# Attention and a two-matrix FFN on one core: batch 2's q and k taken from fp16 copies in DRAM by transposed loads, with a new order of steps

## The chip, the cores and the metric

One of the eight cores of a Trainium2 chip runs the kernel. The metric is the device time of one execution in microseconds. A core has a matrix engine (TensorE, PE in the profile; its weight loads are PEld), VectorE (DVE), ScalarE (ACT), GpSimd (POOL) and SyncE (SP), which run side by side, each taking its own instructions in program order. POOL, SP and ACT also issue the transfers between DRAM and the on-chip memory, which 16 DMA engines carry out.

## The reference

```
scores = (q @ k^T) / 8                        # 8 batches, 12 heads, 448 tokens, 64 channels
attn   = exp(scores) / (1 + sum exp(scores))  # as it comes out: the maximum cancels
x      = (attn @ v), heads side by side       # 3584 tokens x 768
out    = relu(x @ w_in)^2 @ w_out             # w_in 768 x 2048, w_out 2048 x 768
```

All inputs and the output are float32 in DRAM. The kernel computes in fp16 with float32 sums.

## The kernel before

The scores of a head need q and k with the 64 channels on partitions. They come by two ways. Batches 0, 1 and 2 (`ON_PE`) are loaded in their natural form, four heads at a time (a "quad" g: heads 2g, 2g+1, 2g+6 and 2g+7, so three quads to a batch), with a cast to fp16 in the load (`load_quad`, POOL's queue). TensorE transposes each quad of q or k in 14 instructions (`transpose_one`, step `T`), and DVE or ACT copies the result out of PSUM into the batch's tile `qk` (`transposed_copy`, step `U`). Batches 3 to 7 go through DRAM: `stage(b)` (POOL's queue) casts a batch of q and of k into the fp16 buffers `stage_q` and `stage_k`, and `transposed_loads(b)` (SP's queue) reads them back transposed into three planes of `qk`: q, k, and k shifted by one row, so that two tokens stand side by side on the 128 partitions. `tail_keys(b)` then gathers each head's last keys with four POOL copies into `flatq`. `qk` has two buffers, so a batch's planes take the place of the planes of two batches earlier.

A visit of `quad_scores` (step `s`) makes 64 keys' scores for the four heads of a quad against all 448 queries: four matmuls of 448 columns for a batch of `ON_PE`, eight of 224 for the others. `quad_exp` (`e`) is the exponential on ACT, `add_quad` (`a`) sums on DVE, `sums_of_quad` (`S`), `quad_z` (`Z`) and `quad_reciprocal` (`M`) make the denominator, `values_step` (`v`) multiplies with v and `quad_x` (`X`) writes x. The scores go through two PSUM buffers, so a visit waits for the exponential of the visit two before it. Batch 0 does the same in halves of 224 queries, with steps of its own (`p` for the values, `y` for the sums, `z`, `n`, `x`); visits 0 to 23 are batch 0's, 24 to 44 batch 1's, 45 to 65 batch 2's. The first FFN product is `half_in` (`i`) for batch 0 and `later_in` (`j`) for the rest, `relu` (`r`, `k`) and `squared` (`g`, `l`) follow, and `out_piece` (`o`) with `out_done` (`O`) or `out_first` and `out_second` (`O`, `Q`) make and store the output.

There are no loops that schedule: the string `ORDER` lists the steps from the start to the end of batch 2's attention, and `CYCLE` lists those of one batch, run for b = 3 to 7. In both, each word is a step letter with its arguments, and each engine executes its share in the order of the string. A short tail follows.

`d` in ORDER issues an entry of the list `LOADS`: natural quads (0 to 7), v quads of batches 0 and 1 (8 to 13), v of batch 2 (14), `win` in four pieces of two loads (15 to 18), `wout` in four (19 to 22), `stage(3)` (23) and `load_third` (24), which is `transposed_loads(3)`, `tail_keys(3)`, v of batch 3 and `stage(4)`. All but the transposed loads stand in POOL's queue, in the order of the string. In CYCLE a single `d0`, near the end, does this for the next batches:

```
def following():
    if b + 1 < B:
        transposed_loads(b + 1)
        tail_keys(b + 1)
        load_v_quads(b + 1)
        if b + 2 < B:
            stage(b + 2)
```

Most matmuls are recorded under one helper line, L92 (`mm`); L198 are the transposes of `T`, L245 the exponentials, L208 and L206 the copies of `U`, L163 the transposed loads, L179 the copies of `tail_keys`, L154 the staging loads, L116 the natural quads, L104, L102 and L110 the loads of v, L134 `win`, L138 `wout`, L531 the output stores.

Of the kernel before, what the change touches and what calls it, by code (L numbers as in the profile page):

```python
# [16 lines left out]
def kernel(  # L17
# [142 lines left out]
    def transposed_loads(b):  # L160
        qk = qks[b] = qk_pool.tile([128, 3, COLS], FP16, name="qk")
        for i, n, x, c in ((0, "q", FRONT, H * S // 2), (1, "k", FRONT, H * S // 2), (2, "k", 0, COLS)):
            nc.sync.dma_start(  # L163
                out=qk[:, i, 0:c],
                in_=stages[n, b][x:x + c * 2 * D].rearrange("(r c) -> r c", c=2 * D),
                transpose=True,
            )
# [494 lines left out]
    ORDER = """
        d0 W8 c1,4,0 c0,0,1 c1,0,1 t0,0,0 c0,4,1 t1,0,0 u0,0,0,0 t1,0,4 u1,0,0,0 t0,0,4 u1,0,4,0 s0 d8 d1 u0,0,4,0 t0,1,0 e0 t1,1,0 u0,1,0,0 u1,1,0,0 s1 s2 e1
        d10 t0,1,4 u0,1,4,0 t1,1,4 u1,1,4,1 T0,1,0 T0,1,1 s3 U0,1,0,0,4,0 e2 U0,1,1,0,4,0 s4 U0,1,0,4,7,1 e3 d9 U0,1,1,4,7,0 d2 p0 e4 p2 s16 p1 e16 b0,0 b0,1
        p3 b0,2 b0,3 s6 y0 d18 s5 T0,2,0 e6 U0,2,0,0,4,0 z0 T0,2,1 U0,2,1,0,4,0 e5 U0,2,1,4,7,0 U0,2,0,4,7,0 s7 s9 b1,0 n0 b1,1 e7 x0 s8 p4 e9 b1,2 d3 b1,3 p5
        e8 p6 p7 s10 y1 b2,0 p8 p9 e10 s11 p10 b2,1 z1 e11 b2,2 b2,3 s12 p11 s13 n1 x1 y2 e12 T1,0,0 U1,0,0,0,7,0 T1,0,1 z2 n2 s14 e13 x2 p12 p13 s15
        U1,0,1,0,7,0 e14 e15 s17 p14 b3,0 b3,1 e17 s18 i0,7 d17 d5 b3,2 e18 b3,3 p15 y3 z3 b4,0 r0,7,0 s21 s19 e21 T1,1,1 d4 n3 b4,1 i0,6 U1,1,1,0,7,0 s20 d15
        T1,1,0 x3 b4,2 e19 b4,3 d16 s23 p16 p17 p18 r0,6,0 U1,1,0,0,7,0 e20 b5,0 e23 s22 e22 b5,1 p19 y4 s26 z4 n4 i0,4 g0,7 x4 r0,4,0 s27 i0,5 g0,6 b5,2 e26
        s25 e27 T1,2,1 s28 e25 p20 p21 r0,5,0 p22 s24 g0,5 b5,3 e28 d11 T1,2,0 p23 e24 s29 y5 e29 U1,2,1,0,7,0 U1,2,0,0,7,0 T2,0,0 T2,0,1 U2,0,0,0,7,0 z5 g0,4
        d6 U2,0,1,0,7,0 s30 n5 s32 a0,0 e30 d13 i0,0 i0,1 s33 x5 e32 r0,0,0 g0,0 r0,1,0 s31 i1,0 d12 g0,1 e33 i0,3 r1,0,0 e31 r0,3,1 s35 d7 s36 e35 P0 e36  # L670
        i0,2 s34 e34 a0,1 a0,2 g1,0 v0,0 a0,3 S0 v0,1 v0,2 v0,3 v0,4 Z0 v0,5 v0,6 M0 r0,2,0 g0,3 g0,2 s37 i1,3 a1,0 a1,1 e37 X0 r1,3,0 a1,2 g1,3 i1,6 s39 s40
        a1,3 e39 i1,1 r1,1,0 r1,6,0 s43 T2,2,0 e40 d20 T2,2,1 g1,6 e43 s42 g1,1 e42 U2,2,0,0,7,0 s41 d19 i1,5 r1,5,0 e41 s38 e38 T2,1,0 T2,1,1 U2,2,1,0,7,0
        U2,1,0,0,7,1 S1 a2,0 Z1 s44 U2,1,1,0,7,0 i1,4 i1,2 a2,1 e44 r1,4,1 s45 a2,2 g1,5 a2,3 v1,0 v1,1 M1 v1,2 v1,3 v1,4 v1,5 v1,6 r1,2,1 v2,0 S2 v2,1 X1
        g1,4 e45 g1,2 v2,2 v2,3 v2,4 Z2 v2,5 v2,6 M2 s47 X2 s46 i1,7 j3,0,2 r1,7,0 o0,0,4 j3,2,4 j1,0,2 j3,4,6 k3,0 j12,0,2 o0,4,8 j1,2,4 o0,8,12 e46 e47
        o0,12,16 s50 d21 g1,7 s51 j12,2,4 j1,4,6 k1,0 j5,0,2 e51 e50 l3 j5,2,4 j5,4,6 d23 O0,1 k5,1 j12,4,6 l5 o1,0,4 s48 s49 j6,0,2 e49 l1 e48 d22 k12,1 l12
        o1,4,8 o1,8,12 o1,12,16 s53 s52 e52 e53 j6,2,4 j10,0,2 o5,0,4 j6,4,6 O1,1 s55 k6,0 s54 j10,2,4 o5,4,8 j0,0,2 e55 a3,0 j10,4,6 j8,0,2 o5,8,12 j0,2,4
        a3,1 k10,1 o5,12,16 e54 s61 s57 l6 a4,0 j14,0,2 O5,0 e57 j14,2,4 j14,4,6 e61 j8,2,4 a3,2 j9,0,2 j9,2,4 j0,4,6 j9,4,6 a3,3 j8,4,6 l10 s56 k0,0 k14,0
        e56 l0 k8,1 s58 o2,0,4 o2,4,8 l14 d14 s59 v4,0 v4,1 v4,2 v4,3 a4,1 v4,4 v4,5 e58 k9,0 s60 e59 s64 o2,8,12 d24 l9 o2,12,16 a4,2 a4,3 j7,0,2 e60 v4,6
        e64 S4 Z4 M4 O2,0 S3 j7,2,4 o4,0,4 l8 o4,4,8 o4,8,12 o4,12,16 j7,4,6 Z3 s62 X4 s63 M3 O4,0 v3,0 v3,1 v3,2 v3,3 v3,4 v3,5 e62 v3,6 s65 X3 k7,1 j4,0,2
        e65 o3,0,4 a5,0 o3,4,8 o3,8,12 o3,12,16 j15,0,2 j4,2,4 j4,4,6 l7 e63 j15,2,4 a5,1 j2,0,2 O3,1 a5,2 j2,2,4 a5,3 j15,4,6 k4,0 j13,0,2 j11,0,2 S5 Z5  # L680
        k15,0 M5 l4 l15 j2,4,6 k2,0 j13,2,4 l2 j11,2,4 j13,4,6 j11,4,6 k11,1 k13,1 l11 l13
    """
# [35 lines left out]

    CYCLE = """
# [5 lines left out]
        e3,1 o4,2,4 o6,14,16 s3,2 e3,3 o4,4,6 O6,1 a2,2 o4,6,8 s3,5 a2,3 o4,8,10 Q6 o4,10,12 e3,2 e3,5 o4,12,14 o4,14,16 O4,1 Q4 a3,0 s3,6 v2,0 v2,1
        S2 Z2 v2,2 v2,3 v2,4 v2,5 M2 v2,6 e3,6 X2 j2,0,2 j2,2,4 j2,4,6 k2,0 j13,0,2 j13,2,4 l2 j13,4,6 j3,0,2 k13,1 l13 j3,2,4 j15,0,2 j12,0,2 j15,2,4
        j0,0,2 j3,4,6 a3,1 j15,4,6 k3,1 a3,2 k15,1 j12,2,4 a3,3 l15 j0,2,4 j0,4,6 l3 j12,4,6 j10,0,2 j10,2,4 j4,0,2 k0,0 l0 k12,1 l12 j10,4,6 j6,0,2
        j7,0,2 j7,2,4 j7,4,6 j4,2,4 k10,0 j6,2,4 j4,4,6 l10 j6,4,6 k7,1 j5,0,2 l7 j5,2,4 k4,1 j11,0,2 k6,0 j11,2,4 j11,4,6 j9,0,2 l6 j5,4,6 l4 j9,2,4
        j8,0,2 j8,2,4 k5,1 j9,4,6 l5 j1,0,2 k11,0 j8,4,6 j1,2,4 j1,4,6 k9,1 j14,0,2 j14,2,4 l11 l9 k8,0 j14,4,6 l8 k1,1 l1 k14,0 S3 Z3 d0 l14 M3
# [61 lines left out]
```

## Time and profile before

| | |
|---|---|
| median of 3 runs | 396.51 us (396.07 to 397.43) |
| the profiled execution, its own time | 396.87 us |
| its span, first to last instruction | 394.8 us |
| PE busy | 385.5 us, 98% |
| DVE / ACT / POOL busy | 240.5 / 238.1 / 59.8 us |
| transposes of `T` on TensorE (L198) | 224, of them 84 for batch 2 |
| HBM read / written | 45.69 / 17.93 MB |
| granted TensorE clock | 1.00 |

The page gives busy times of each engine, the chain of work that ended last, followed back from the last instruction, and the costliest groups of instructions. The timeline lists instructions in order of time; a row has start, length, engine, line, operation, what is written and read, and in brackets the idle time before it and what ended it. The DMA view lists the queues (q0 is POOL's queue, q1 SP's) with packets, megabytes and the time that their packets took as a share of 16 engines, and the issues with the time from issue to landing. The windows view gives for a stretch the busy time and instruction count of each engine (PE, PEld, DVE, ACT, POOL), the granted clock, the DMA engines' share and GB/s (bytes as written). A busy PE isn't PE at its peak, since matmuls overlap: a step's cost is read from start to start.

### The profile page before, as it was taken

To read this page: it belongs to the slowest core of one execution; us is meant where nothing else is said; L and a number is where in the kernel's file an instruction comes from. 1 tells how busy PE (TensorE), PEld (TensorE's weight loads), DVE (VectorE), ACT (ScalarE), POOL (GpSimd) and SP (SyncE) were. 2 spreads that over 40 slices of the span, in tenths; PEclk is the share of its full clock that TensorE was granted. 3 is DMA by queue.
4 is the path that set the end of the run, shared out by engine and by line. 5 is a ranking of instruction groups with operands and counts; after the bars stand their busy time and mean duration, and the time that the engine had idled before them with its cause. 6 is when DMAs were issued, how large, how long until landed. Compare 5 with 4: busy or idle time off the path is not lost.

```text
span 394.8 us, 13877 instructions
## 1 busy us (share of the span) xinstructions
PE 385.5 (98%) x6252; PEld 262.9 (67%) x6252; DVE 240.5 (61%) x445; ACT 238.1 (60%) x324; POOL 59.8 (15%) x96
## 2 busy tenths in 40 slices
PE   8789999999999999999999999999999999999997
PEld 4567776445599766896579866776677765555665
DVE  3889994385746765668536876567646785285000
ACT  4999895768479625895279834896269934100111
POOL 8354500003200032000500016000500000000000
PEclk9999999999999999999999999999999999999999
DMA  8999999568942579419692398527652100100222
GB/s 146 203 204 206 203 206 208 98 127 154 191 85 63 113 140 181 96 43 161 113 203 75 77 193 127 129 64 141 126 74 68 58 7 2 62 0 14 68 80 81
DMA packets 75051, 45.33 MB, mean 115 GB/s; under 512 B 47472, under 2 KB 72944, under 8 KB 74992
## 3 DMA queue, kind: packets, MB, share of 16 engines
q0 software_dynamic: 24752, 22.62, 36.3%
q1 hardware_dynamic: 49952, 21.59, 25.0%
q8 instruction: 49, 0.80, 0.8%
q10 hardware_dynamic: 288, 0.23, 0.2%
q14 instruction: 10, 0.08, 0.1%
HBM read 45.69 MB, written 17.93 MB: 161 GB/s over the span
## 4 chain that ended last, share of the span: by engine, by line
PE 94%; DVE 3%; ACT 1%; issue 1%; DVEq 0%; ACTq 0%
PE mp L92 81%; PE sp L92 9%; PE xp L92 2%; PE mp L198 2%; ACT et L245 1%; DVE qk L208 1%; DVE half L334 1%; DVE half L332 0%; PE mp L225 0%; ACT rcp L356 0%; ACT rcp L363 0%; DVE qk L235 0%; DVE half L338 0%; DVE half L336 0%; DVE rt L496 0%
## 5 line engine op out<-in xcount | busy, mean ns | idle before, releaser
L92 PE MATMUL mp<-wout,gs 64*64 64x384 f16 (+2 forms) x2592 | 166.7, 322 | 0.0
L92 PE MATMUL mp<-xt,win 128*64 128x448 f16 (+2 forms) x1344 | 151.4, 339 | 0.1
L245 ACT ACTIVATE et<-sp 128x896 f16<-128x896 f32 (+1 forms) x131 | 110.8, 889 | 30.1 <-PE sp L92 28.9
L92 PEld LDWEIGHTS <-win 128*64 128x64 f16 (+1 forms) x1344 | 89.6, 106 | 58.7 <-issue 7.4
L92 PEld LDWEIGHTS <-gs 64*64 64x64 f16 (+1 forms) x2592 | 105.9, 106 | 34.3 <-issue 1.1
L494 ACT ACTIVATE rt<-mp 128x448 f16<-128x448 f32 x55 | 29.3, 544 | 57.2 <-PE mp L92 52.4
L500 DVE TENSOR_TENSOR gs<-rt 128x448 f16<-128x448 f16 x128 | 49.2, 401 | 22.2 <-ACT rt L494 19.8
L92 PE MATMUL sp<-qk 64*64 64x224 f16 (+1 forms) x1056 | 57.4, 274 | 2.5 <-issue 0.9
L496 DVE TENSOR_SCALAR rt<-mp 128x448 f16<-128x448 f32 x73 | 45.2, 621 | 23.0 <-PE mp L92 21.5
L557 ACT ACTIVATE ot<-mp 128x384 f32<-128x384 f32 (+2 forms) x34 | 16.4, 481 | 51.3 <-PE mp L92 50.8
L92 PEld LDWEIGHTS <-qk 64*64 64x64 f16 x1056 | 36.1, 114 | 14.4 <-issue 7.4
L179 POOL COPY flatq<-qk 64x384 f16<-64x384 f16 x20 | 12.4, 643 | 205.9 <-DMA qk<-stage_k 205.6
L245 ACT ACTIVATE nn<-sp 128x896 f16<-128x896 f32 x42 | 36.7, 915 | 1.9 <-PE sp L92 1.8
L478 DVE TENSOR_TENSOR xt<-mp,rcp 128x448 f16<-128x448 f32 x42 | 24.3, 620 | 20.0 <-ACT rcp L457 17.8
L92 PEld LDWEIGHTS <-vn 64*64 64x64 f16 x756 | 24.1, 107 | 9.8 <-issue 2.6
L563 DVE SCALAR_TENSOR_TENSOR ot<-mp,ot 128x384 f32<-128x384 f32 x35 | 19.5, 556 | 16.9 <-ACT ot L557 15.3
L454 ACT ACTIVATE rcp<-sp,one_b 128x896 f32<-128x896 f32 x21 | 21.2, 1007 | 10.0 <-PE sp L92 10.0
L92 PE MATMUL mp<-et,vn 64*64 64x448 f16 (+1 forms) x448 | 25.1, 343 | 0.0
L559 DVE TENSOR_SCALAR ot<-mp 128x384 f32<-128x384 f32 x23 | 12.8, 556 | 19.6 <-PE mp L92 19.5
L432 DVE TENSOR_TENSOR half<-et 128x1792 f16<-128x1792 f16 x15 | 16.3, 1087 | 7.0 <-ACT et L245 6.9
L457 ACT ACTIVATE rcp<-rcp 128x896 f32<-128x896 f32 x21 | 20.0, 952 | 0.6
L434 DVE TENSOR_TENSOR half<-half,et 128x1792 f16<-128x1792 f16 x15 | 16.4, 1091 | 0.7 <-ACT et L245 0.3
(59 smaller groups left out, 198.2 us busy)
## 6 DMA issues: line engine op xcount, KB each, us to landing
out_dram<-ot SPq DMA_DIRECT2D x52, 96.0 KB, 2.3
out_dram<-ot SPq DMA_DIRECT2D x19, 192.0 KB, 1.9
win<-in_moe_w_in_dram POOLq DMA_DIRECT2D x8, 384.0 KB, 11.1
wout<-in_moe_w_out_dram POOLq DMA_DIRECT2D x4, 768.0 KB, 15.6
vn<-in_v_dram POOLq DMA_DIRECT2D x10, 288.0 KB, 4.8
stage_q<-in_q_dram POOLq DMA_DIRECT2D x4, 676.0 KB, 8.8
stage_k<-in_k_dram POOLq DMA_DIRECT2D x4, 676.0 KB, 12.0
nn<-in_q_dram POOLq DMA_DIRECT2D x8, 224.0 KB, 8.1
```

The source lines that it names most:

```text
L92: return nc.tensor.matmul(out_, lhsT, rhs, start=start, stop=stop)
L245: nc.scalar.activation(out=out_, in_=in_, func=AF.Exp, scale=scale)
L432: nc.vector.tensor_add(esq[m], a[:, 0:w], a[:, w:2 * w])
L434: nc.vector.tensor_add(esq[m], esq[m], z[:, 0:w])
L454: nc.scalar.activation(out=rcp, in_=zp[:, :, 0:S], func=AF.Ln, bias=one_b)
L457: nc.scalar.activation(out=zqs[m], in_=zqs[m], func=AF.Exp, scale=-1.0)
L478: nc.vector.tensor_mul(xts[b][:, 2 * g + i, :], xqs[m][i][:, 0:S], zqs[m][:, i, :])
L494: nc.scalar.activation(out=rt[:, 0:m], in_=hp[:, 0:m], func=AF.Relu)
L496: nc.vector.tensor_scalar(out=rt[:, 0:m], in0=hp[:, 0:m], scalar1=0.0, scalar2=None, op0=ALU.max)
L500: nc.vector.tensor_mul(gs[:, f0:f0 + per, t0 % RING:t0 % RING + n], r, r)
L557: nc.scalar.activation(out=ot, in_=op[:, 0:w], func=AF.Copy, scale=OUT_SCALE)
L563: nc.vector.scalar_tensor_tensor(out=ot, in0=lo[:, 0:w], scalar=OUT_SCALE, in1=ot, op0=ALU.mult, op1=ALU.add)
```

## The change

Batch 2 leaves `ON_PE`. Its six natural quads are no longer loaded, and its six pairs of `T` and `U` steps go; instead `LOADS` has `stage(2)` (d5), `transposed_loads(2)` (d6) and `tail_keys(2)` (d7). Its scores, exponentials and output stores take the form of the later batches. v of batch 2 is loaded in the later batches' layout. `ORDER` is a new list of the remaining steps: among the loads, the natural quads of batches 0 and 1 come earlier, all four `wout` loads come ahead of `stage(3)`, and `stage(2)` stands behind `win`; among TensorE's steps the order of score visits, of the FFN's pieces and of the outputs differs throughout.

A batch's following loads are cut into six steps and a seventh for the staging: one transposed load each (d0 to d2; now first the two of k, then q), the two copies of `tail_keys` that read one plane (d3, d4), v (d5) and `stage(b + 2)` (d6). In CYCLE they stand after `Q4`, in the order d0 d3 d6 d1 d4 d2 d5. The rest of CYCLE is as it was.

```diff
-    ON_PE = (0, 1, 2)
+    ON_PE = (0, 1)
...
+    PLANES = (("k", FRONT, H * S // 2), ("k", 0, COLS), ("q", FRONT, H * S // 2))
+
+    def transposed_load(b, i):
+        qk = qk_of(b)
+        n, x, c = PLANES[i]
+        nc.sync.dma_start(
+            out=qk[:, (i + 1) % 3, 0:c],
+            in_=stages[n, b][x:x + c * 2 * D].rearrange("(r c) -> r c", c=2 * D),
+            transpose=True,
+        )
+
     def transposed_loads(b):
-        qk = qks[b] = qk_pool.tile([128, 3, COLS], FP16, name="qk")
-        for i, n, x, c in ((0, "q", FRONT, H * S // 2), (1, "k", FRONT, H * S // 2), (2, "k", 0, COLS)):
...
+        for i in range(3):
+            transposed_load(b, i)
...
-    def tail_keys(b):
+    def tail_keys(b, planes=(1, 2)):
...
-    LOADS = ([lambda b=b, g=g: load_quad(b, g) for b in range(3) for g in range(NQ) if b + g]
-             + [lambda b=b, g=g: load_v_quads(b, g, g + 1) for b in range(2) for g in range(NQ)]
+    LOADS = ([lambda b=b, g=g: load_quad(b, g) for b in ON_PE for g in range(NQ) if b + g]
+             + [lambda: stage(2), lambda: transposed_loads(2), lambda: tail_keys(2)]
+             + [lambda b=b, g=g: load_v_quads(b, g, g + 1) for b in ON_PE for g in range(NQ)]
              + [lambda: load_v_quads(2)]
...
-        def following():
+        def following(n):
             if b + 1 < B:
-                transposed_loads(b + 1)
-                tail_keys(b + 1)
-                load_v_quads(b + 1)
-                if b + 2 < B:
+                if n < 3:
+                    transposed_load(b + 1, n)
+                elif n < 5:
+                    tail_keys(b + 1, (n - 2,))
+                elif n == 5:
+                    load_v_quads(b + 1)
+                elif b + 2 < B:
                     stage(b + 2)
```

The loads stand in the two ORDERs in this sequence (in after's list of LOADS 0 to 4 are natural quads, 5 to 7 are batch 2's staging, transposed loads and tail keys, and 8 to 24 are what they were):

```
before: d0 d8 d1 d10 d9 d2 d18 d3 d17 d5 d4 d15 d16 d11 d6 d13 d12 d7 d20 d19 d21 d23 d22 d14 d24
after:  d0 d1 d8 d9 d2 d10 d3 d18 d17 d15 d4 d16 d11 d13 d5 d19 d20 d22 d12 d21 d6 d7 d23 d14 d24
```

The first score visit of batch 2 is s45 in before's ORDER. In after's it is s53, the second visit of batch 2's second quad, and it stands here:

```
S1 Z1 M1 v1,0 v1,1 v1,2 v1,3 v1,4 v1,5 v1,6 s44 O0,0 a2,0 e44 O4,0 s53 o2,0,4 d7 o2,4,8
```

More of the change, by code (lines that the diff above doesn't have):

```diff
@@ L158, in stage @@
                                     in_=src[0:lo + TOTAL - hi].rearrange("(r w) -> r w", r=1))
-    def transposed_loads(b):
-        qk = qks[b] = qk_pool.tile([128, 3, COLS], FP16, name="qk")
-        for i, n, x, c in ((0, "q", FRONT, H * S // 2), (1, "k", FRONT, H * S // 2), (2, "k", 0, COLS)):
[L163 to L167, printed above, removed]
-    kms = {}
-    def tail_keys(b):
-        km = kms[b] = flat.tile([128, H, 64], FP16, name="flatq")
-        for r in range(2):
-            for odd in range(2):
+    PLANES = (("k", FRONT, H * S // 2), ("k", 0, COLS), ("q", FRONT, H * S // 2))
[7 more added lines that the diff above has]
+        )
+    def transposed_loads(b):
+        for i in range(3):
+            transposed_load(b, i)
+    kms = {}
+    def tail_keys(b, planes=(1, 2)):
+        if b not in kms:
+            kms[b] = flat.tile([128, H, 64], FP16, name="flatq")
+        km = kms[b]
+        for which in planes:
+            for r in range(2):
                 rows_ = slice(64 * r, 64 * r + 64)
-                which, x = (1, 0) if odd == r else (2, odd)
+                odd, x = (r, 0) if which == 1 else (1 - r, 1 - r)
                 src = qks[b][rows_, which, x:x + H * S // 2].rearrange("p (h x) -> p h x", h=H)
@@ L600, in load_quad @@
     def load_quad(b, g):
-        x = {(0, 1): (0, 0), (0, 2): (0, 1), (1, 0): (1, 0), (1, 1): (0, 0), (1, 2): (0, 1),
-             (2, 0): (1, 0), (2, 1): (1, 1), (2, 2): (0, 0)}[b, g]
+        x = {(0, 1): (0, 0), (0, 2): (0, 1), (1, 0): (1, 0), (1, 1): (0, 0), (1, 2): (0, 1)}[b, g]
         if (b, x[0]) not in nats:
@@ L662 @@
     ORDER = """
[L663 to L678, printed above, removed]
@@ L679 @@
-        e64 S4 Z4 M4 O2,0 S3 j7,2,4 o4,0,4 l8 o4,4,8 o4,8,12 o4,12,16 j7,4,6 Z3 s62 X4 s63 M3 O4,0 v3,0 v3,1 v3,2 v3,3 v3,4 v3,5 e62 v3,6 s65 X3 k7,1 j4,0,2
-        e65 o3,0,4 a5,0 o3,4,8 o3,8,12 o3,12,16 j15,0,2 j4,2,4 j4,4,6 l7 e63 j15,2,4 a5,1 j2,0,2 O3,1 a5,2 j2,2,4 a5,3 j15,4,6 k4,0 j13,0,2 j11,0,2 S5 Z5
-        k15,0 M5 l4 l15 j2,4,6 k2,0 j13,2,4 l2 j11,2,4 j13,4,6 j11,4,6 k11,1 k13,1 l11 l13
+        d0 c1,4,0 c0,0,1 W8 t0,0,0 c1,0,1 u0,0,0,0 t1,0,0 t1,0,4 c0,4,1 u1,0,0,0 t0,0,4 u1,0,4,1 s0 t0,1,0 u0,0,4,0 d1 e0 u0,1,0,0 t1,1,0 u1,1,0,0 s1
@@ new lines @@
+        s2 t0,1,4 e1 u0,1,4,0 t1,1,4 u1,1,4,0 e2 T0,1,1 T0,1,0 s3 U0,1,1,0,4,0 d8 U0,1,0,0,4,0 e3 d9 U0,1,1,4,7,0 s5 T0,2,0 d2 s6 U0,1,0,4,7,0 b0,0
+        T0,2,1 U0,2,0,0,4,0 U0,2,1,0,4,0 d10 e5 s4 e6 U0,2,0,4,7,0 p0 U0,2,1,4,7,0 e4 s7 e7 p2 d3 p1 s9 b0,1 e9 s8 b1,0 p3 d18 b0,2 e8 b1,1 s10 b1,2
+        b0,3 T1,0,0 y0 b2,0 d17 s14 T1,0,1 b1,3 e10 z0 U1,0,1,0,7,0 s13 e14 U1,0,0,0,7,0 b2,1 n0 e13 s12 x0 p4 d15 p5 d4 p6 d16 p7 e12 y1 s11 z1 s15
+        d11 p8 e11 b2,2 b3,0 p9 s19 p10 b2,3 n1 p11 e15 y2 x1 z2 d13 T1,1,1 T1,1,0 s17 n2 e19 s16 e17 d5 b3,1 U1,1,1,0,7,0 x2 b3,2 p12 b3,3 e16 p13
@@ new lines @@
+        p14 s18 p15 b4,0 y3 U1,1,0,0,7,0 e18 z3 i0,6 n3 s21 e21 x3 s20 e20 i0,7 r0,6,0 s24 d19 p16 e24 p17 b4,1 p18 p19 b4,2 g0,6 r0,7,0 s22 d20 i0,5
+        b5,0 e22 g0,7 s26 e26 s27 b5,1 i0,4 s23 e27 b4,3 r0,5,0 b5,2 e23 y4 b5,3 i0,0 z4 r0,4,0 s30 n4 s25 g0,5 i0,1 x4 e30 e25 r0,0,0 g0,4 r0,1,0 s29
+        T1,2,1 a0,0 p20 g0,1 s28 d22 e29 e28 d12 d21 U1,2,1,0,7,0 p21 g0,0 p22 p23 s33 y5 z5 T1,2,0 U1,2,0,0,7,0 n5 e33 x5 s32 i0,3 i1,4 r0,3,0 r1,4,0
+        g0,3 i0,2 g1,4 e32 a0,1 r0,2,1 s31 P0 s35 e35 g0,2 a0,2 i1,6 r1,6,0 i1,2 e31 i1,0 g1,6 r1,2,1 r1,0,0 s37 a0,3 s34 e34 i1,3 g1,0 g1,2 i1,1 e37
@@ new lines @@
+        r1,1,1 r1,3,1 v0,0 v0,1 S0 v0,2 v0,3 Z0 v0,4 v0,5 d6 v0,6 s36 i1,5 a1,0 e36 s40 M0 g1,1 e40 s39 i1,7 r1,5,1 g1,3 a1,1 X0 r1,7,0 o0,0,4 a1,2
+        o4,0,4 s42 g1,7 e39 s43 o0,4,8 e43 a1,3 o4,4,8 e42 g1,5 o4,8,12 s38 s41 o0,8,12 o0,12,16 e41 o4,12,16 e38 S1 Z1 M1 v1,0 v1,1 v1,2 v1,3 v1,4
+        v1,5 v1,6 s44 O0,0 a2,0 e44 O4,0 s53 o2,0,4 d7 o2,4,8 o2,8,12 a2,1 o2,12,16 X1 a2,2 v2,0 a2,3 S2 e53 Z2 v2,1 O2,0 v2,2 v2,3 M2 v2,4 v2,5 v2,6
+        X2 s52 s54 e54 o5,0,4 j13,0,2 o5,4,8 e52 o5,8,12 s49 s45 j13,2,4 e49 j13,4,6 k13,0 j9,0,2 l13 d23 o5,12,16 e45 j9,2,4 j12,0,2 j12,2,4 O5,0 s56
@@ new lines @@
+        s48 e56 j12,4,6 j4,0,2 j9,4,6 k12,0 j4,2,4 j5,0,2 k9,1 j5,2,4 l12 j4,4,6 j5,4,6 e48 s46 e46 s51 e51 j7,0,2 k5,0 j11,0,2 l9 j11,2,4 j11,4,6
+        j7,2,4 s57 e57 k4,0 s55 l4 j2,0,2 d14 j3,0,2 j2,2,4 j3,2,4 j7,4,6 l5 e55 k11,0 l11 k7,1 j2,4,6 a4,0 a4,1 s47 s50 e47 j6,0,2 o3,0,4 o3,4,8 l7
+        j3,4,6 s59 e50 k2,1 e59 s58 k3,0 a3,0 e58 o1,0,4 o3,8,12 j8,0,2 a4,2 j8,2,4 j8,4,6 d24 j6,2,4 l2 o3,12,16 j6,4,6 k6,0 s61 a3,1 s60 e61 O3,1
+        o1,4,8 l3 o1,8,12 e60 a4,3 o1,12,16 l6 s62 S4 k8,0 e62 O1,0 l8 v4,0 v4,1 v4,2 v4,3 a5,0 v4,4 v4,5 v4,6 Z4 a3,2 M4 s64 e64 j1,0,2 j15,0,2
@@ L682 @@
+        j1,2,4 j1,4,6 X4 j15,2,4 s63 e63 j15,4,6 j14,0,2 j14,2,4 s65 a3,3 a5,1 S3 k15,1 j0,0,2 k1,1 j10,0,2 e65 a5,2 Z3 j14,4,6 j10,2,4 l1 l15 j0,2,4
+        j0,4,6 k14,0 j10,4,6 v3,0 l14 v3,1 v3,2 a5,3 M3 v3,3 k0,1 S5 k10,1 l0 v3,4 v3,5 Z5 v3,6 l10 X3 M5
     """
@@ L715, in cycle @@
             "Q": lambda n: out_second(128 * ((first + n) // 2), HALF * ((first + n) % 2), HALF),
-            "d": lambda n: following(),
+            "d": lambda n: following(n),
         }
@@ L724 @@
         v1,2 v1,3 M1 v1,4 O5,0 v1,5 Q5 v1,6 X1 o6,0,2 s3,4 e3,4 o6,2,4 s3,0 e3,0 o6,4,6 o6,6,8 a2,0 o6,8,10 o6,10,12 s3,1 o4,0,2 o6,12,14 a2,1 s3,3
[L725 to L729, printed above, removed]
+        e3,1 o4,2,4 o6,14,16 s3,2 e3,3 o4,4,6 O6,1 a2,2 o4,6,8 s3,5 a2,3 o4,8,10 Q6 o4,10,12 e3,2 e3,5 o4,12,14 o4,14,16 O4,1 Q4 d0 d3 d6 d1 d4 d2 d5
+        a3,0 s3,6 v2,0 v2,1 S2 Z2 v2,2 v2,3 v2,4 v2,5 M2 v2,6 e3,6 X2 j2,0,2 j2,2,4 j2,4,6 k2,0 j13,0,2 j13,2,4 l2 j13,4,6 j3,0,2 k13,1 l13 j3,2,4
+        j15,0,2 j12,0,2 j15,2,4 j0,0,2 j3,4,6 a3,1 j15,4,6 k3,1 a3,2 k15,1 j12,2,4 a3,3 l15 j0,2,4 j0,4,6 l3 j12,4,6 j10,0,2 j10,2,4 j4,0,2 k0,0 l0
+        k12,1 l12 j10,4,6 j6,0,2 j7,0,2 j7,2,4 j7,4,6 j4,2,4 k10,0 j6,2,4 j4,4,6 l10 j6,4,6 k7,1 j5,0,2 l7 j5,2,4 k4,1 j11,0,2 k6,0 j11,2,4 j11,4,6
+        j9,0,2 l6 j5,4,6 l4 j9,2,4 j8,0,2 j8,2,4 k5,1 j9,4,6 l5 j1,0,2 k11,0 j8,4,6 j1,2,4 j1,4,6 k9,1 j14,0,2 j14,2,4 l11 l9 k8,0 j14,4,6 l8 k1,1 l1
+        k14,0 S3 Z3 l14 M3
     """
```

## The prediction

> **What bounds the kernel now.** I read the page first: totals and the chain that ended last.
>
> ```profile
> span 394.8 us, 13877 instructions
> ...
> PE 385.5 (98%) x6252; PEld 262.9 (67%) x6252; DVE 240.5 (61%) x445; ACT 238.1 (60%) x324; POOL 59.8 (15%) x96
> ...
> PE 94%; DVE 3%; ACT 1%; issue 1%; DVEq 0%; ACTq 0%
> ```
>
> TensorE is the chain. The profiled execution took 396.87 us: this span and 2.07 us around it, 0.36 above the median of 396.51. Next TensorE's timeline, for its last waits.
>
> ```profile
> 22.92 0.58 PE L92 MATMUL xp<-et,vn 64*64 64x224 f16 x16 [0.88 <-DVE xt L371]
> 23.30 0.29 PE L92 MATMUL sp<-qk 64*64 64x224 f16 x4
> 23.87 0.39 PE L92 MATMUL sp<-qk 64*64 64x224 f16 x8 [0.28 <-ACT et L245]
> 24.06 0.39 PE L92 MATMUL xp<-et,vn 64*64 64x224 f16 x8
> 24.30 0.39 PE L92 MATMUL sp<-qk 64*64 64x224 f16 x8
> 24.62 1.32 PE L92 MATMUL mp<-xt,win 128*128 128x224 f16 x12
> ```
>
> From 24.62 on its time is the sum of its steps, start to start in the same timeline: an `i` step 1.21 (two in 47.11 to 49.52), `o` of four pieces 0.67, `j` of two 0.39, `T` 0.45 (two in 51.59 to 52.49), a score visit `s` 0.26, `v` and `p` 0.19, `S` 0.23, `y` 0.15. ORDER from `i0,7` on has 16 i, 24 o, 48 j, 10 T, 47 s, 44 v and p, 6 S, 3 y: 81.3, so 24.6 + 81.3 = 105.9, and the timeline has CYCLE's first matmul at 105.91. Before 24.62 ACT sets the pace: busy without a gap from 9.11. Then the stretches, for the DMA engines (the last two columns are their share and GB/s):
>
> ```profile
> 20.00:40.00 20.00, 18.54 (x387) 14.55 (x380) 17.61 (x37) 19.27 (x28) 10.38 (x15) 1.00 1.25 204
> 40.00:66.00 26.00, 25.87 (x357) 18.90 (x355) 22.87 (x43) 21.39 (x27) 5.58 (x7) 1.00 1.24 206
> ```
>
> They are full until 66 us at 205 GB/s: POOL's loads stand in one queue. So a load's landing follows from the bytes ahead of it. The DMA issues in narrow windows give issue to landing:
>
> ```profile
> win<-in_moe_w_in_dram POOLq DMA_DIRECT2D x1, 384.0 KB, 11.9
> stage_q<-in_q_dram POOLq DMA_DIRECT2D x1, 676.0 KB, 19.1
> stage_k<-in_k_dram POOLq DMA_DIRECT2D x1, 676.0 KB, 21.3
> ```
>
> Issued at 28.57, 43.95 and 45.03, they land at 40.5, 63.0 and 66.3: 3.25 us a staging copy. Likewise three `wout` loads land 3.9 apart, and 224 KB take 1.1.
>
> **Part by part. Batch 2's transposes.** Six T go: 6 x 0.45 = 2.7 us of TensorE, and 5 DVE copies (0.62) and one on ACT (0.91), which TensorE does not wait for. The 21 score visits become eight matmuls of 224 columns for four of 448: the same columns; CYCLE's visits of this form take 0.21 against 0.26, so 0 to -1.0, and I take 0, as here FFN matmuls follow them.
>
> **The new front.** TensorE's first `i` is now `i0,6`. The visit ahead of it, s18, waits for e17; ACT has 19.2 us of work up to there by the old durations, and runs 5.2 behind that sum (e17 in before: 19.05 of work ahead, start 24.30): 24.4, and with s18, p15 and y3 `i0,6` starts at 25.0. Its `win` piece is due at 24.6 by bytes, later ones within 0.4 to 1.0 ahead of their use. From there ORDER has 77.0 us of steps (16 i, 24 o, 48 j, 2 T, 46 s, 43 v and p, 6 S, 2 y): it would end at 102.1, 3.8 earlier, if nothing else waited. If ACT or `win` lag, 1 us of that goes.
>
> **Staged q and k of batch 2.** Fifteen loads of 224 KB and eight of 384 KB stand ahead of d5, just as many as before has up to the `win` load that lands at 40.5; two staging copies later it is 47.0. The first transposed load cannot start before (its slot is free after s23, at 32). Behind d5 in POOL's queue stand four `wout` loads and a v quad: 4 x 3.9 + 1.1 = 16.7, alone until 63.7. The transposed loads come on SP's queue into the same 16 DMA engines; in before they ran with none of POOL's loads beside them:
>
> ```profile
> GB/s 213 112 183 137 12 206 288 292 279 280 256 267 290 183 212 262 197 237 276 230 291 288 207 185 245 229 173 156 284 279 291 289 283 125 0 6 9 28 396 15
> ...
> qk<-stage_k SPq DMA_TRANSPOSE x2, 5.8
> ```
>
> Issued at 83.60, the last landed at 95.5: 11.9 us for 2.07 MB, with gaps; the plateau of 290 GB/s gives 7.1. In ORDER the first visit of batch 2 is s53, and it reads all three planes. From `i0,6` to s53 there are 37.2 us of steps (16 i, 25 s, 14 v, 8 o, 8 p, 2 T, 2 S, 2 y), so TensorE is there at 62.2. By then the DMA engines would have to move 16.7 and 7.1 to 11.9 in 15.2 us. What a load on SP's queue gets beside POOL's loads, an output store shows, issued at 100.81 (the others of that size land in 2.3); the second line is the queues from 101 to 104.4:
>
> ```profile
> out_dram<-ot SPq DMA_DIRECT2D x1, 96.0 KB, 6.6
> q0 software_dynamic: 1211, 0.62, 137.0%
> ```
>
> In 3.4 us not one packet of q1. From 105 to 107.5 it gets 22.6% of the engines and POOL's queue falls to 85.4%, so the two add up and don't hide each other. So I let the planes wait until POOL's loads are through: 63.7 + 7.1 = 70.8 at the plateau, 75.6 at the old pace. I take 71.5, nearer the first, since the loads are by then queued and start without the first gap. s53 waits 62.2 to 71.5: 9.3 us. From s53 to ORDER's end stand 39.9 us (48 j, 16 o, 21 s, 21 v, 4 S): 71.5 + 39.9 = 111.4, against 105.9: +5.5 (+4.8 to +9.6). The 2.7 and the front's gain are inside this: the wait takes them whole.
>
> **Behind it.** tail_keys(2) waits on POOL for two planes; behind it are stage(3), v of batch 2 and load_third. Staging then starts near 73 and lands near 80, the transposed loads of batch 3 near 95 with v beside them; CYCLE reads them at 113: hidden by 18 us. SP's next stores come behind the transposed loads; `ot` has four buffers: nothing.
>
> **CYCLE.** On SP `d` stands where it stood, behind Q4's stores. On POOL stage(b+2) now follows the first plane's copies, ahead of v. v lands some 7 us later than 153.9 and is read at 169.4: hidden. Staging ends ahead of the next cycle, where in before this stands (chain in 160 to 164):
>
> ```profile
> 161.45 0.09 PE sp L92
> 161.54 0.88 issue
> 162.41 0.40 PE sp L92 x7
> ```
>
> TensorE's weight loads stood for 1.17 there, waiting for no other engine, until the staging copy landed at 162.2: I book -1.2 (0 to -1.2). But staging now runs beside the second and third planes: the first lands at 138.8, copies take 1.2, staging 6.5 until some 148, and the last plane, some 3.6 behind, lands near 151.6; the next cycle reads it at 152.5. In the next two cycles the margin is about nothing: 0 to 1.5 each in three cycles, and I take 1.2 in all. CYCLE comes to 0 (-1.2 to +4.5).
>
> Sum: 396.87 + 5.5 + 0 = 402.4 for a run like the profiled one; less 0.36, **402.0**.
>
> **Rivals.** *Even sharing.* If transposed loads get half of the engines, they are done 14.2 us after 47.0, at 61.2, before s53; then the v quad of d12, behind three `wout` (12.8 of work in all), lands at 47.0 + 12.8 + 7.1 = 66.9, and v1,0 (due 60.6) waits. ORDER ends at 66.9 + 41.5 (s53's rest and v1,0 to s44) = 108.4: +2.5, with CYCLE's code wait gone 397.8. The store's missing packets speak against it, though a store has four packets an engine and a plane 168. [...]
>
> *Hidden: faster.* The planes move in small packets (8240 of 8496 in that window are under 512 B), POOL's loads in larger ones; they might be held up by different things. If both ran at full pace, planes would land by 58.9 and `wout` and v on time: ORDER ends at 102.1, -3.8, and -1.2 in CYCLE: 391.5. It holds if less than 3 of the 7.1 to 11.9 us adds to POOL's queue. Against it: q0 falling as q1 gets on.
>
> *CYCLE turns slower.* The planes wait for staging by over 2 us in each of three cycles on top: above 407.
>
> *The change doesn't do what it says.* If POOL's queue ran lighter than its bytes say, by 5 us or more at d5, s53 waits 4 and the gains pay for it: 396 to 397.
>
> **How the numbers follow.** Forecast 0.62; even sharing 0.14, half of it within 0.3% (about what a measurement of this kernel can tell from no change); hidden 0.12; CYCLE slower 0.07; light queue 0.05, nearly all within 0.3%. Slower 0.77, same 0.10, faster 0.13. The range: from 396.5, under even sharing, to 406.5, the old pace of the planes with CYCLE at +1; left out are the hidden case and the top of CYCLE's.
>
> **What would show it.** Right: a wait of 6 to 13 us on TensorE at the first eight score matmuls on planes of batch 2, ended by DMA qk, near 62 us; transposes x140 left; ORDER's end near 111; no code wait of 1 us early in a cycle. Even sharing: the wait stands at `mp<-et,vn` instead, ended by DMA vn. Wrong: no wait over 1 us near 62 us.

## The result, and the profile after

| | before | after |
|---|---|---|
| median | 396.29 us (4 runs, 396.04 to 397.43) | 418.81 us (4 runs, 413.58 to 422.88) |
| the profiled execution, its span | 396.87, 394.8 us | 420.73, 418.9 us |
| ORDER's end (CYCLE's first matmul) | 105.91 us | 118.34 us |
| granted clock | 1.00 | 0.976 |

After is slower: ratio 1.0472, 95% interval 1.0393 to 1.0552, against 402.0 predicted (396.5 to 406.5). The ratio is of the two faster runs (413.58 and 416.9, at a mean clock of 0.983 and 0.979); the profile is of a longer run (0.976), so its terms are larger than the ratio's.

The page first: span, busy times, the clock granted to TensorE in 40 slices, the chain that ended last.

```profile
span 418.9 us, 13874 instructions
...
PE 391.0 (93%) x6252; PEld 260.0 (62%) x6252; DVE 239.0 (57%) x441; ACT 237.6 (57%) x322; POOL 61.4 (15%) x99
...
PEclk9999997699999999899998999999999999999999
...
PE 75%; DMA 12%; SPq 7%; ACT 3%; POOL 1%; issue 1%; DVE 0%; POOLq 0%; ACTq 0%
```

TensorE held 94% of the chain before and holds 75% now; DMA and SP's queue, which issues the transposed loads, hold 19%. The dips of the clock, in slices 7, 8, 17 and 22, are new as well. The waits (engine and line, what was waited for, us in total, times, longest) say for which transfers:

```profile
PE sp L92 <- DMA qk<-stage_q: 17.3, 3, 7.4
PE mp L92 <- DMA vn<-in_v_dram: 3.1, 1, 3.1
```

`qk<-stage_q` is the last of the three planes. TensorE's timeline shows where: in ORDER at v1,0 and at s53, then at the first visit of the next batch in the second and the third turn of CYCLE.

```profile
61.39 0.38 PE L92 MATMUL sp<-half,ones 64*64 64x448 f16 x4
64.86 2.82 PE L92 MATMUL mp<-et,vn 64*64 64x448 f16 x28 [3.09 <-DMA vn<-in_v_dram]
67.48 0.40 PE L92 MATMUL sp<-qk 64*64 64x448 f16 x4
75.29 0.59 PE L92 MATMUL sp<-qk 64*64 64x224 f16 x8 [7.42 <-DMA qk<-stage_q]
75.82 5.30 PE L92 MATMUL mp<-wout,gs 128*128 128x384 f16 x16
...
118.34 1.49 PE L92 MATMUL mp<-nn,vn 64*64 64x448 f16 x28
...
163.51 1.49 PE L92 MATMUL mp<-nn,vn 64*64 64x448 f16 x28
170.67 0.59 PE L92 MATMUL sp<-qk 64*64 64x224 f16 x8 [5.67 <-DMA qk<-stage_q]
...
215.84 1.49 PE L92 MATMUL mp<-nn,vn 64*64 64x448 f16 x28
221.55 0.59 PE L92 MATMUL sp<-qk 64*64 64x224 f16 x8 [4.21 <-DMA qk<-stage_q]
...
266.88 1.49 PE L92 MATMUL mp<-nn,vn 64*64 64x448 f16 x28
```

The rows `mp<-nn,vn` are the starts of CYCLE's turns. The first turn takes 45.17 us (118.34 to 163.51), the second 52.33, the third 51.04. In before they are 45.23, 46.34 and 45.34. Look also at the row of 75.82: the 16 matmuls of o2 take 5.30 us, 0.33 each, where before's four of an `o` step stood 0.67 apart, 0.17 each. They run right after the wait, and the windows view says at which clock (columns as before: busy time and count of PE, PEld, DVE, ACT, POOL; clock; DMA share; GB/s):

```profile
61.00:75.00 14.00, 3.79 (x39) 1.49 (x37) 5.51 (x8) 3.06 (x4) 3.68 (x6) 0.73 1.27 179
75.00:82.00 7.00, 6.71 (x44) 3.11 (x48) 0.56 (x1) 1.18 (x2) 2.65 (x5) 0.56 1.00 193
82.00:110.00 28.00, 28.00 (x311) 15.05 (x302) 16.74 (x30) 18.90 (x24) 6.45 (x10) 1.00 1.07 175
...
171.00:176.00 5.00, 5.00 (x112) 4.07 (x107) 0.48 (x1) 1.72 (x2) 0.00 (x0) 0.76 0.00 0
...
222.00:227.00 5.00, 5.00 (x104) 4.08 (x100) 0.44 (x1) 1.68 (x2) 0.00 (x0) 0.74 0.09 14
```

So the waits for qk each have two prices: the time that TensorE stands, and work at a lower clock behind it (0.56, 0.76 and 0.74 on average in these windows).

The DMA view shows who had the engines, here in the windows 48 to 57, 57 to 64, 64 to 70.3 and 70.3 to 75 us (packets, MB, share of 16 engines; q0 is POOL's queue, q1 SP's):

```profile
q0 software_dynamic: 1964, 1.48, 106.2%
q1 hardware_dynamic: 1026, 0.26, 22.4%
...
q0 software_dynamic: 1076, 0.83, 90.9%
q1 hardware_dynamic: 1077, 0.28, 42.5%
...
q1 hardware_dynamic: 1768, 0.44, 76.8%
q0 software_dynamic: 695, 0.52, 52.7%
...
q1 hardware_dynamic: 4363, 1.17, 118.7%
```

The transposed loads are not shut out, as the prediction had it. They get a fifth of the engines, then a third, then more than half, and about half of their bytes move in the last five us, with POOL's queue empty. The two shares add up to between 119% and 133% all the time.

Sum, from before's span of 394.8: ORDER +12.43 (118.34 against 105.91), the second and third turn of CYCLE +7.16 and +5.87 over the undisturbed 45.17, the stand of 1.17 us in before's second turn (the prediction's code wait) -1.17: 419.1, against 418.9.

### The profile page after: what moved, and what is told of

It reads as the page before. It is cut to its first block, busy times and chain, and to the rows that moved or that the text cites. A ratio compares the mean times of both kernels' runs of the same rounds, so it can differ in the third digit from the quotient of the medians.

```text
span 418.9 us, 13874 instructions
## 1 busy us (share of the span) xinstructions
PE 391.0 (93%) x6252; PEld 260.0 (62%) x6252; DVE 239.0 (57%) x441; ACT 237.6 (57%) x322; POOL 61.4 (15%) x99
## 4 chain that ended last, share of the span: by engine, by line
PE 75%; DMA 12%; SPq 7%; ACT 3%; POOL 1%; issue 1%; DVE 0%; POOLq 0%; ACTq 0%
PE mp L92 66%; DMA qk<-stage_q 10%; PE sp L92 8%; SPq L165 6%; DMA nn<-in_q_dram 2%; ACT et L253 1%; POOL nn L116 1%; PE xp L92 1%; ACT rt L502 0%; SPq L539 0%; ACT rcp L371 0%; PE mp L206 0%; POOL vn L104 0%; ACT ot L565 0%; DVE ot L571 0%
## 5 line engine op out<-in xcount | busy, mean ns | idle before, releaser
L92 PE MATMUL mp<-wout,gs 64*64 64x384 f16 (+2 forms) x2592 | 170.7, 328 | 0.0
L92 PEld LDWEIGHTS <-gs 64*64 64x64 f16 (+1 forms) x2592 | 103.7, 108 | 38.1 <-issue 4.2
L92 PE MATMUL sp<-qk 64*64 64x224 f16 (+1 forms) x1116 | 55.0, 269 | 19.3 <-DMA qk<-stage_q 17.3
L508 DVE TENSOR_TENSOR gs<-rt 128x448 f16<-128x448 f16 x128 | 50.7, 412 | 19.8 <-ACT rt L502 17.0
L504 DVE TENSOR_SCALAR rt<-mp 128x448 f16<-128x448 f32 x71 | 44.0, 620 | 21.9 <-PE mp L92 20.2
L92 PEld LDWEIGHTS <-qk 64*64 64x64 f16 x1116 | 34.6, 116 | 34.0 <-issue 27.0
L187 POOL COPY flatq<-qk 64x384 f16<-64x384 f16 x24 | 15.8, 658 | 222.1 <-DMA qk<-stage_k 177.4
L567 DVE TENSOR_SCALAR ot<-mp 128x384 f32<-128x384 f32 x25 | 13.9, 555 | 44.7 <-PE mp L92 44.7
L486 DVE TENSOR_TENSOR xt<-mp,rcp 128x448 f16<-128x448 f32 x42 | 24.2, 619 | 21.8 <-ACT rcp L465 17.6
L92 PEld LDWEIGHTS <-vn 64*64 64x64 f16 x756 | 22.3, 109 | 14.6 <-DMA vn<-in_v_dram 3.8
L92 PE MATMUL mp<-et,vn 64*64 64x448 f16 (+1 forms) x448 | 26.5, 359 | 3.3 <-DMA vn<-in_v_dram 3.1
## 6 DMA issues: line engine op xcount, KB each, us to landing
stage_k<-in_k_dram POOLq DMA_DIRECT2D x5, 676.0 KB, 11.9
```

What stands on the lines that cost most here:

```text
L92: return nc.tensor.matmul(out_, lhsT, rhs, start=start, stop=stop)
L486: nc.vector.tensor_mul(xts[b][:, 2 * g + i, :], xqs[m][i][:, 0:S], zqs[m][:, i, :])
L504: nc.vector.tensor_scalar(out=rt[:, 0:m], in0=hp[:, 0:m], scalar1=0.0, scalar2=None, op0=ALU.max)
L508: nc.vector.tensor_mul(gs[:, f0:f0 + per, t0 % RING:t0 % RING + n], r, r)
```

## The experiments

The theory: the transposed loads and POOL's loads share 16 DMA engines, and whatever of POOL's is in its queue when the transposed loads are issued makes the last plane late; what stands in that queue is set by the order of steps. One rival: the transposed loads are slow by themselves, or cost wherever they are put. Another: CYCLE's six steps cost by being split or moved, not by what their transfers meet.

**CYCLE's staging back to the end (e1_stage_last).** All of after, but in CYCLE:

```
- d0 d3 d6 d1 d4 d2 d5
+ d0 d1 d2 d3 d4 d5 d6
```

> The changed kernel, with stage(b+2) put last among CYCLE's d steps again (d0 d1 d2 d3 d4 d5 d6 at the same place). Queue theory: a transposed load on SP's queue gets little of the DMA engines while POOL's loads are queued, so the third plane's waits in CYCLE (5.9 and 4.5 us in the changed kernel's profile, landing 18 us after issue) go, and the half-clock stretches behind them (1.4 and 1.5 us) with them; the waits near 61 and 67 us stay: 405 to 409 us. Order theory (CYCLE is only late because ORDER is): the waits in CYCLE stay, 413 to 420.

Measured: 406.6 us (406.32 to 409.45), ratio to before 1.0272, 1.0227 to 1.0317. TensorE's waits of over 0.5 us for transfers of qk or v in its profile:

```profile
PE sp L92 <- DMA qk<-stage_q: 8.6, 1, 8.6
PE mp L92 <- DMA vn<-in_v_dram: 2.4, 1, 2.4
```

They are ORDER's two; its turns of CYCLE take 45.17 each. So CYCLE's new order holds all of the difference, 7 us against after's fastest run and 12 against its median, and ORDER the other 10.

**CYCLE's order alone (e2_cycle_alone).** Before, with after's `transposed_load`, `tail_keys` and CYCLE; batch 2 stays with TensorE.

> The kernel before, with the new CYCLE and its six steps alone (ORDER, ON_PE and LOADS as before). Queue theory: waits at the third plane of 2 to 7 us in up to three cycles, each with up to 3.4 us at half clock behind it: 399 to 408 us. Order theory: no such waits, and without the code wait at 161 us 395 to 397.

Measured: 404.63 us (402.14 to 411.98), ratio 1.0185, 1.0132 to 1.0238: slower by itself. TensorE's waits for transfers of qk or v, in a profile of its longest run, with a mean clock of 0.988 (the others had 0.992 and 0.996, so less of the half clock):

```profile
PE sp L92 <- DMA qk<-stage_q: 11.6, 2, 7.4
```

And its issues from 139 to 160 us, with the time to landing:

```profile
stage_q<-in_q_dram POOLq DMA_DIRECT2D x1, 676.0 KB, 8.7
stage_k<-in_k_dram POOLq DMA_DIRECT2D x1, 676.0 KB, 10.8
vn<-in_v_dram POOLq DMA_DIRECT2D x2, 288.0 KB, 10.2
...
qk<-stage_q SPq DMA_TRANSPOSE x1, 17.6
```

The third plane, issued at 140.1, landed at 157.8, and the last of POOL's loads, v, at 158.1. In before the third plane took 5.8. Here it lands as POOL's queue runs dry.

**Staging one step later (e7_stage_fourth).** The same as e2, but staging behind the second plane's copies on POOL, not the first's:

```
- d0 d3 d6 d1 d4 d2 d5
+ d0 d3 d1 d4 d6 d2 d5
```

> The kernel before with CYCLE's six steps in the order d0 d3 d1 d4 d6 d2 d5: staging behind the second plane's copies, not the first's. Queue theory: the third plane is issued at about 140 and lands at 145 to 147 in the first cycle, hardly later than in before, since the staging copies are issued only at about 145; no wait by DMA qk, staging through some 6.5 us later (about 152), so the code wait of 1.2 us in 161 to 164 goes: 395 to 397 us. Rival (that the six steps stand earlier or are split is itself what costs): like the run of CYCLE alone, 400 to 408.

Measured: 395.59 us (394.92 to 396.91, 12 runs), ratio 0.9964, 0.9948 to 0.9979: faster than before, and the best version of this study. POOL waits for the second plane (143.7) before it issues staging, at 145.1; by then the third plane is nearly through:

```profile
stage_q<-in_q_dram POOLq DMA_DIRECT2D x1, 676.0 KB, 6.0
...
qk<-stage_q SPq DMA_TRANSPOSE x1, 5.7
```

5.7 us to landing against 17.6, from one word moved two places. The steps are split as in e2 and stand where e2's stand, so the rival that splitting or moving them costs falls. Four turns of CYCLE take 45.17 to 45.19 each (107.00, 152.19, 197.36, 242.53, 287.70): that stand of before's second turn is gone, as computed, and its 1.2 us fit the gain of 1.1 in the medians. They are not shown to be that gain: in this profile ORDER ended 1.1 later than in before's (107.00 against 105.91, with a wait of 0.4 for a k load near 10 us), and the span is 0.3 shorter.

**The half clock (e3_fill).** e1 with dummy matmuls, 14 before v1,0 and 38 before s53, so that TensorE works where it would wait:

```
- Z1 M1 v1,0           - O4,0 s53
+ Z1 M1 f14 v1,0       + O4,0 f38 s53
```

> As e1_stage_last, with matmuls on a constant ahead of the two waits in ORDER: 14 before v1,0 and 38 before s53 (0.19 us each, 2.6 and 7.1 us), into PSUM tiles that nothing reads. If the half clock after a wait is caused by TensorE standing still, no stretch at 0.5 is left near 64 and 71 us, and it is 3 to 4.5 us faster than e1_stage_last although it does more work. If the clock falls for another reason (DMA load, total power), the stretches stay and it is equal to e1_stage_last or up to 2 us slower.

Measured: 404.26 us (404.13 to 404.76), ratio 1.0199, 1.017 to 1.0228. Stretches from 61, 75 and 82 us, as shown of after:

```profile
61.00:75.00 14.00, 12.82 (x99) 6.28 (x99) 4.88 (x8) 2.94 (x4) 4.21 (x8) 1.00 1.18 187
75.00:82.00 7.00, 7.00 (x82) 3.97 (x80) 1.71 (x3) 4.42 (x5) 1.88 (x3) 1.00 1.05 211
```

Clock 1.00, and 82 matmuls where after does 44 in the same 7 us. s53 starts as late as in e1 (74.38 against 74.19), yet from there to ORDER's end it is 40.4 us against 43.3 (114.77 and 117.45). So 2.9 us of ORDER's loss in the profile, 2.3 in the medians, came from TensorE having stood still, and not from the transfers.

**Less in POOL's queue (e4_half_wout).** e1 without d21 and d22, the `wout` loads of the second half of the output's columns; that half is multiplied with the first half's weights:

```
- mm(op[:, 0:w], g, wout[:, fb, n0:n0 + w], ...)
+ mm(op[:, 0:w], g, wout[:, fb, n0 % HALF:n0 % HALF + w], ...)
```

> As e1_stage_last, with the second half of wout's columns neither loaded nor read (both halves of the output use the first): the two loads of d21 and d22, 7.8 us of POOL's queue, are left out. Queue theory: the planes of batch 2 land near 66 instead of 75, the v quad near 58, the wait at s53 falls from 7.9 to under 3 us and the one at v1,0 goes: 397 to 401 us. Rival, the transposed loads are slow by themselves when three are issued in a row this early: the last still lands at 73 to 75, the wait at s53 is 8 to 11 us, 404 to 408.

Measured: 397.82 us (395.34 to 399.78, 10 runs), ratio 1.0032, 1.0007 to 1.0058. With 7.8 us of loads gone the last plane lands at 67.6, not 74.2, and the wait falls:

```profile
PE sp L92 <- DMA qk<-stage_q: 2.7, 1, 2.7
```

The same transposed loads on the same path: the rival that they are slow by themselves falls. What stands in POOL's queue sets the wait here: 8.6 us in e1, 2.7 without those loads.

**Loads in another order, visits later (e5_later).** e1 with these moves in ORDER, and the plane of q loaded first:

```
- s28 d22 e29 e28 d12 d21 U1,2,1      + s28 d12 e29 e28 U1,2,1
- v0,5 d6 v0,6                        + v0,5 d6 d7 d21 d22 v0,6
- O4,0 s53 o2,0,4 d7 ... X2 s52       + O4,0 o2,0,4 ... X2 o2,12,16 s53 s52 e53
  (o5 from behind X2 to behind e51; d14 ahead of d23)
```

> The kernel after with the queue emptied for the transposed loads: the v quad ahead of the later wout loads, the two wout loads for the second half of the columns and what reads them moved behind batch 2's tail copies on GpSimd's queue, s53 and e53 moved behind X2, CYCLE's staging last, the plane of q loaded first. Queue theory: nothing of GpSimd's stands beside the transposed loads after about 56 us, so the planes land at 63 to 67; TensorE comes to s53 at about 67 and waits 0 to 1.5; no stretch at half clock near 70; ORDER ends at 103 to 105; CYCLE without waits: 391.5 to 394.5 us. Rival (the transposed loads are slow by themselves, or the front's gain of 3.8 us is not there): a wait at s53 of 3 us or more or a later arrival, 396 to 399.

Measured: 398.89 us (397.26 to 400.62, 12 runs), ratio 1.0051, 1.0032 to 1.0071. The waits are what the theory says: the planes land at 66.65, TensorE is at s53 at 68.97, and no wait for qk is left. The time is what the rival says, and ORDER ends at 107.15. In its place stand short waits:

```profile
66.77 0.38 PE L92 MATMUL sp<-half,ones 64*64 64x448 f16 x4 [0.83 <-DVE half L446]
...
70.39 0.40 PE L92 MATMUL sp<-qk 64*64 64x224 f16 x8 [0.82 <-ACT et L253]
...
71.81 0.40 PE L92 MATMUL sp<-qk 64*64 64x224 f16 x8 [0.53 <-ACT et L253]
72.61 0.40 PE L92 MATMUL sp<-qk 64*64 64x224 f16 x8 [0.41 <-ACT et L253]
```

With steps pulled together behind the planes, S2 waits for DVE and the visits for ACT's exponentials. Between the prediction's 102.1 for an ORDER without waits and 107.15 lie: `i0,6` at 25.87 and not 25.0, and TensorE's waits of 0.83, 0.82, 0.53 and 0.41 here and 0.21 at 58 us: 3.7 of 5.05. The rest is open.

**Staging ahead of v (e8_stage_ahead_of_v).** e5 with `d6 d5` for `d5 d6` in CYCLE.

> e5_later with staging ahead of v in CYCLE (d0 d1 d2 d3 d4 d6 d5): all planes have landed before either is issued. Queue theory: no wait by DMA qk; staging ends about 3 us earlier than in e5_later, so a code wait early in a cycle, if e5_later has one, is smaller; v lands some 13 us after its planes' copies and is read over 10 us later: 0 to -1.2 us against e5_later. Rival (staging anywhere ahead of v costs): +4 or more against e5_later, with waits by DMA vn in CYCLE.

Measured: 400.02 us (398.0 to 401.89, 7 runs), ratio 1.0073, 1.0042 to 1.0104. CYCLE has no wait for qk or v, so the rival's sign isn't there; the difference from e5 is within the intervals. But the profiled run shows something else, near 9 us, in the windows 8 to 10.2 and 10.2 to 13.6:

```profile
8.00:10.20 2.20, 0.70 (x14) 0.36 (x9) 0.64 (x2) 1.18 (x3) 1.31 (x2) 1.00 1.16 175
10.20:13.60 3.40, 3.33 (x66) 2.23 (x66) 2.19 (x6) 1.60 (x3) 0.00 (x0) 0.66 1.26 200
```

TensorE waited 1.6 us for a k load ahead of the first T, and then worked at a clock of 0.66; its `i0,6` started at 27.42. In e5's profiled run that wait was 0.8, the clock stayed whole, and `i0,6` started at 25.87.

**Dummies at the first wait, steps put apart (e9_later_filled, e10_later_front_filled).** e10 is e5 with `W5`, five dummy matmuls, ahead of the first T. e9 has also s53 and s52 ahead of `o2,14,16`, with two `j` steps between most of the score visits behind them.

> e5_later with five 512-column dummy matmuls (W5) ahead of the first T, where TensorE waits 0.8 to 1.6 us for a k load near 9 us, and with steps between X1 and s48 put apart so that S2 does not wait for DVE and the score visits not for ACT. Theory (a stand of TensorE near 9 us is followed by half clock for 3.4 us in some runs, and e5_later lost some 3 us to short waits in 65 to 73): no half clock early, i0,6 at 25.5 to 26, ORDER's end at 104.5 to 106, 394 to 396.5 us and a spread of its runs under 2 us. Rival (the spread and the loss come from the DMA queue's order in each run, not from the clock): as e5_later, 397 to 400.5, or slower by the 1 us that the dummies take.

> e5_later with W5 ahead of the first T alone, nothing else moved. Theory (half clock after the wait near 9 us): the profile near e5_later's own 397.3 (its clock there was whole), and the slow tail of e5_later's runs (to 400.6) gone: median 396.5 to 397.8. Rival (queue order): median 398 to 400.

Measured: e9 398.54 us (397.04 to 401.56, 9 runs), ratio 1.006, 1.0034 to 1.0085; e10 399.32 us (398.26 to 401.0, 6 runs), ratio 1.0077, 1.0055 to 1.0099. Both miss, at the rival's times. The dummies did what they were for: in both profiles the clock is whole to 21 us. But `i0,6` starts no earlier in e9 (26.21), and ORDER ends at 106.76; it waits 0.9 us for `wout` at 80 us, where e5 waited 0.2 at 58 us. In e10 the half clock came at another place, behind four short stands (windows 69 to 73 and 73 to 76.5):

```profile
69.00:73.00 4.00, 2.24 (x35) 0.96 (x28) 1.45 (x3) 3.46 (x5) 4.00 (x6) 0.92 0.89 120
73.00:76.50 3.50, 3.50 (x12) 1.35 (x10) 1.02 (x2) 0.80 (x1) 0.68 (x2) 0.61 1.26 218
```

In e9, whose visits are put apart, the same windows show 1.00. That e9 is still not faster stays open: neither the front's later start nor all of the spread of its runs is explained.

## Why the prediction was wrong

The sign and ORDER's mechanism were right; two terms of the sum were too small, and CYCLE's was the larger miss.

| step | predicted | after's profile |
|---|---|---|
| the staged copies of batch 2 landed | 47.0 us | 47.4 |
| POOL's loads behind them through | 63.7 | 70.3 |
| the last plane landed, and s53 began | 71.5 | 75.2, 75.3 |
| TensorE comes to v1,0 | 60.6 | 61.5 |
| from s53 to ORDER's end | 39.9 | 43.1 |
| ORDER | +5.5 | +12.4 |
| CYCLE | 0 (-1.2 to +4.5) | +11.9 |

**The front** held to 0.9 us: TensorE came to v1,0 at 61.5. Its gain, and that of the T's, went into the wait, as the prediction said.

**s53's wait: the mechanism right, 3.8 us too small.** The failed choice is "71.5, nearer the first": the plateau of 290 GB/s for the planes. The upper end, 75.6 at the old pace, is near what came. Counted from staging's landing, the planes took 11.0 us beyond the 16.7 of POOL's loads (47.42 to 75.16), and in e4 9.8 beyond 8.9 (48.94 to 67.65): between the plateau's 7.1 and the old 11.9, so that 75.6 came this near is in part luck. The order was wrong too: the planes did move beside POOL's loads, which so ended 6.6 late. That is why v1,0 waited too, as the rival of even sharing had it for the v quad; but its other half, planes done at 61.2, did not come, and s53's later release takes the wait for v whole. Why the store of 100.81 in before got no packet in 3.4 us, where the planes got a fifth, no run here shows. A steady half of the engines for the planes, the term of the rival of even sharing, no run shows: from 48 to 57 us q1 had 22.4% against 106.2% of the time, with 1026 packets to 1964 of q0, and from 57 to 64 us 42.5% against 90.9%, with 1077 to 1076. So equal numbers of packets were not equal shares here.

**From s53 to ORDER's end: 3.1 us that had no term.** "39.9 us" was a sum of steps at full clock. 75.3 to 81.2 ran at half, and e3 shows that this is the price of having stood. 3.8 and 3.1 make up the 6.9 by which ORDER's term failed.

**CYCLE: the step that failed most.** The prediction priced the third plane as "some 3.6 behind" staging and landing at 151.6, 0.9 ahead of its reader, and booked 1.2 for three turns. In after the third plane was issued at 152.13, and staging at 152.34 and 152.87. Staging alone was to take 6.5 us; with the planes beside it, it took 10.6 (to 162.9). And v, whose turn on POOL comes at the second plane's copies, was issued at 156.8, into POOL's queue, ahead of most of the third plane. The queues from 157 to 163 us and from 163 to 170.5 us, and the plane's time to landing:

```profile
q0 software_dynamic: 451, 1.10, 93.9%
q1 hardware_dynamic: 455, 0.12, 14.3%
...
q0 software_dynamic: 1485, 0.60, 71.3%
q1 hardware_dynamic: 1732, 0.44, 59.5%
...
qk<-stage_q SPq DMA_TRANSPOSE x1, 18.5
```

From 157 to 163 us the two queues had equal numbers of packets, but q1's were small: 0.12 MB against 1.10. The plane landed at 170.6, v at 170.3, and TensorE had stood since 165.0. The prediction had seen v behind staging and called it "hidden" by looking at its own reader, without adding v to what the third plane must wait for. How much of the wait is v's and how much staging's no run separates: in the third turn the plane landed at 221.5, ahead of v's end (226.8) and of the second staging copy's (223.2). Each wait was then followed by a stretch at half clock: turns longer by 7.16 and 5.87 us against waits of 5.67 and 4.21.

**The stand of 1.2 us**, the prediction's code wait, went, in after and in e7: the number was right. Its cause, staging that lands inside the turn, is not shown, and that it came out may be luck: in before's third turn staging landed 11.5 us in (209.02), later than in the second (11.1), and the turn took 45.34; and in e8's profile TensorE stood for 1.28 at 254.3, with staging landed at 251.1.

**The rivals.** CYCLE turning slower was among them, above 407, at a chance of 0.07, with the right mechanism ("the planes wait for staging"): what was missing was v beside staging in what the third plane meets. Hidden transfers, and a queue lighter than its bytes, fall with the first row of after's waits. The range's upper end doesn't follow from its own terms: 75.6 gives 406.1, and with CYCLE at +1 407.1, not 406.5.

## What to carry to other kernels

When a transfer is moved, list every transfer that can be in flight with it on any queue and add their times; the one that is needed first may be the last to land (in e2 the third plane landed at 157.8, with the last of POOL's loads, 158.1). An order of issue that lets the urgent transfer start before the others are in the queue (here one step later on POOL) costs nothing and was worth 9 us (404.63 in e2, 395.59 in e7). Price a long stand of TensorE with the half clock behind it (1.5 and 1.7 us in after's turns, behind waits of 5.67 and 4.21), and look for short stands close together as well (in e10 four of at most 0.88 within 7 us).
